# The order in which matmuls walk through their columns: blocks from the end, in an attention and softplus-MLP kernel

## The chip, the cores and the metric

The kernel runs on one core of one Trainium2 chip. The metric is the device time of one execution, in microseconds, as the median of several runs. Beside it there is one profiled execution, from which every duration below is read.

## What is computed

```python
# q, k, v: (8, 8, 576, 64); g_norm: (64,); w_in: (512, 2048); w_out: (2048, 512); all float32
kv  = einsum('bhsd,bhse->bhde', k, v)
out = einsum('bhsd,bhde->bhse', q, kv)
out = out / sqrt(mean(out * out, axis=-1) + 1e-06) * g_norm
x = out.transpose(0, 2, 1, 3).reshape(8 * 576, 512)      # 4608 tokens x 512
h = x @ w_in
g = softplus(h)                                          # max(h, 0) + log1p(exp(-|h|))
result = g @ w_out                                       # 4608 x 512
```

The attention part is small. Nearly all the arithmetic is in the two products of the MLP, 4608 x 512 x 2048 each.

## The kernel before, in words

Every float32 operand of the two large products is split into three float32r pieces (a high part, the rest scaled up, and a correction), and a product of two such operands is made by three matmuls that add into the same PSUM bank. Each matmul has a weight load of its own: 128 rows by 128 columns of the one operand are loaded into TensorE, and the columns of the other (256, 384 or 512 of them) are streamed past, read from SBUF and added into as many places of a PSUM bank. In the profile the first is LDWEIGHTS (engine PEld) and the second MATMUL (engine PE).

The work has two parts, and both take part of the 2048 middle columns, which stand in 16 chunks of 128.

The *narrow part* (up to about 355 us) goes over 12 blocks of 384 tokens while the attention is still being made. `step(s)` takes one block and one chunk: 64 steps, 4 chunks for each of the first four blocks and 6 for each of the others. `mm1` (L863) makes the 384 columns of h with 12 matmuls: 3 pieces, and for each 4 tiles of the 512 inner values. They all add into one bank, and the loop counter `m` runs from 0 to 11. Softplus and the split into pieces follow on ScalarE and VectorE, and `mm2(i)` (L870) makes the second product, for each of 3 token tiles 3 matmuls of 512 columns.

The *wide part* (from about 338 us to the end) goes over 9 blocks of 512 tokens and takes the other chunks in pairs, 48 wide steps in two phases. `wide_step(k)` makes the first product by a scheme of 7 products in place of 8, each of them on a half of 256 tokens: `product(u, q)` (L1065) has 6 matmuls of 256 columns, 3 pieces (`m`) by 2 inner tiles (`kd`), and adds into a quarter of two banks (`place(q)`). So there are 48 x 7 x 6 = 2016 matmuls of 256 columns. `mm2(c, i)` (L1136) makes the second product, 2 chunks x 4 token tiles x 3 pieces of 512 columns in each wide step, 1152 matmuls in all. Between these stand copies, softplus and splits on ScalarE and VectorE.

The order of all work is made by a planner (`Plan`): every piece of work is a task with an engine, a cost written by hand, a position, and the buffers that it takes and gives. `Plan.order` plays this through and issues the tasks in the order of the starts that it finds. A product is one task of 710 ns, an `mm2` one of 700, an `mm1` one of 2100. These costs don't depend on the way in which a matmul reads its columns.

In the kernel before, only the 256-column products read their columns in an order of their own. `from_the_end` turns an operand of n words into blocks of 4 words and takes the last block first; inside a block the words go forward. It is put on the streamed operand and on the place in PSUM alike, so each column still adds into its own place, and the sum is the same:

```python
return x.rearrange("p (b w) -> p b w", w=4)[:, ::-1]
```

All other matmuls read forward.

Of the kernel before, what the change touches and what calls it, by code (L numbers as in the profile page):

```python
# [9 lines left out]
F32R = mybir.dt.float32r  # L10
# [8 lines left out]
P = 128  # L19
# [19 lines left out]
    return x.rearrange(f"r ({' '.join(names)}) -> r {' '.join(names)}", **dict(zip(names, shape[1:])))  # L39


def from_the_end(x):

    return x.rearrange("p (b w) -> p b w", w=4)[:, ::-1]


class Slot:
# [13 lines left out]
class Plan:  # L61
# [19 lines left out]
    def slot(self, ring):  # L81
        return Slot(ring)

    def add(self, engine, ns, run, after=(), pos=0.0, take=(), give=(), size=0, behind=None, follows=None, kind="all"):
        pos, behind = round(pos, 4), None if behind is None else round(behind, 4)
        t = Task(engine, ns, run, [a for a in after if a is not None], pos, list(take), list(give), size)
        for s in t.give:
            s.readers += 1
        self.tasks.append(t)
        t.follows = follows  # L90
        t.behind = behind
        t.kind = kind
        return t
# [113 lines left out]
def kernel(  # L207
# [24 lines left out]
    nc = tc.nc  # L232
# [5 lines left out]
    KD, KF = d_model // P, d_ff // P  # L238
# [610 lines left out]
    def step(s):  # L849
        n, c = ORDER[s]  # L850
        cs = CHUNKS[n]
        h, g, gv = slot("h"), slot("g"), slot("gv")
        if c == cs[0]:
            sums[:] = [slot(f"s{i}") for i in range(TB)]
        xv, w_in, w_out = xv_slots[n], w_slots[0, c], w_slots[1, c]
        mine = list(sums)
        kept = c >= 4

        def mm1():
            hp = new(h, [P, NT])  # L860
            for m in range(3 * KD):
                i, kd = divmod(m, KD)
                nc.tensor.matmul(hp, lhsT=w_in.tile[:, i, kd * P:(kd + 1) * P], rhs=xv.tile[:, i, kd],  # L863
                                 start=(m == 0), stop=(m == 3 * KD - 1))

        def mm2(i):
            if c == cs[0]:
                new(mine[i], [P, d_model])
            for m in range(3):
                nc.tensor.matmul(mine[i].tile, lhsT=gv.tile[:, m, i * P:(i + 1) * P], rhs=w_out.tile[:, m],  # L870
                                 start=(c == cs[0] and m == 0), stop=(c == cs[-1] and m == 2))

        def low():
            nc.vector.tensor_tensor(out=gv.tile[:, 1], in0=g.tile, in1=gv.tile.bitcast(F32)[:, 0], op=ALU.subtract)

        def less():
            f32 = gv.tile.bitcast(F32)
            nc.vector.scalar_tensor_tensor(out=gv.tile[:, 2], in0=f32[:, 1], scalar=-RADIX, in1=f32[:, 0],
                                           op0=ALU.mult, op1=ALU.add)

        a = add("PE", 2100, mm1, x_split[n] + factors_done[0, c] + [m for _, m in mm1s[-1:]] +
                (factors_done[1, ORDER[s - 2][1]] if s > 1 else []), s, [h],
                ([xv] if c == cs[-1] else []) + ([w_in] if s == last_step[c] and c != 4 else []))
        mm1s.append((s, a))
        a = add("ACT", 490, lambda: nc.scalar.activation(new(g, [P, NT]), h.tile, func=AF.Softplus, scale=1.0 + E),  # L885
                [a], s, [g], [h])
        a = add("ACT", 530, lambda: nc.scalar.activation(new(gv, [P, 3, NT], F32R)[:, 0], g.tile, func=AF.Copy, scale=DOWN),
                [a], s, [gv])
        a = add("DVE", 570, low, [a], s, [], [g])
        a = add("DVE", 570, less, [a], s)  # L890
        for i in range(TB):
            a2 = add("PE", 700, lambda i=i: mm2(i), [a] + factors_done[1, c] + [mm2s.get(i)], s + 1.5,
                     [mine[i]] if c == cs[0] else [],
                     [gv] + ([w_out] if s == last_step[c] and not kept else []))
            mm2s[i] = a2
            if c == cs[-1]:
                leave(0, n * TB + i, mine[i], a2, s + 1.5)
# [145 lines left out]
    def wide_step(k):  # L1043
        ph, n, p = STEPS[k]
        ab, gv = slot("ab"), slot("gvp")
        b = starts[k]
# [3 lines left out]
        mine = list(wide_sums)  # L1050
        outs = [w_slots[1, c] for c in (2 * p, 2 * p + 1)]

        def place(q):
            return ab.tile[:, q // 2, q % 2 * HW:(q % 2 + 1) * HW]
# [3 lines left out]
        def product(u, q):  # L1058
            f, i = PRODUCTS[u]
            w = forms[p][f].tile  # L1060
            dst, v = unit_slots[ph, n, u]
            for m in range(3):
                for kd in range(2):
                    at = i * 2 * P + kd * P
                    nc.tensor.matmul(from_the_end(place(q)), lhsT=w[:, m, at:at + P],  # L1065
                                     rhs=from_the_end(dst.tile[:, m, v, kd] if u < 6 else dst.tile[:, m, kd]),
                                     start=(u == 0 and not m and not kd), stop=(m == 2 and kd == 1), skip_group_check=True)

        def multiply(u, q, after, pos, take=(), follows=None):
            f = PRODUCTS[u][0]  # L1070
            give = [unit_slots[ph, n, u][0]] if last else []
            if final and u in (2, 3, 5, 6):
                give.append(forms[p][f])
            return add("PE", 710, lambda: product(u, q), unit_done[ph, n, u] + forms_done[p][f] + list(after), pos, take, give,
                       follows=follows)
# [3 lines left out]
        def gt(dtype=F32):  # L1079
            if dtype not in held:  # L1080
                held[dtype] = sb.tile([P, 2, WIDE], dtype, tag=f"g{gv.place}", name=f"g{gv.place}_{dtype == F32}")
            return held[dtype]

        def gvt(m, dtype=F32):
            y = gv.tile[:, m]
            return y if dtype == F32R else y.bitcast(F32)
# [8 lines left out]
        def begin():  # L1095
            new(ab, None)
            product(0, X)
# [33 lines left out]
        def mm2(c, i):  # L1131
            fresh = first and not c and ph < LAST
            if fresh:
                new(mine[i], [P, d_model])
            for m in range(3):
                nc.tensor.matmul(mine[i].tile, lhsT=(gvt(m, F32R) if m < 2 else gt(F32R))[:, c, i * P:(i + 1) * P], rhs=outs[c].tile[:, m],  # L1136
                                 start=fresh and not m, stop=(last and c == 1 and m == 2), skip_group_check=True)

        seeds = {}
# [19 lines left out]
        for c in range(2):  # L1159
            for i in range(TW):  # L1160
                slot_pos = b + PACE + MM2[TW * c + i]
                a2 = add("PE", 700, lambda c=c, i=i: mm2(c, i),
                         [split_done[c]] + factors_done[1, 2 * p + c] + ([seeds[i]] if i in seeds and not c else []) +
                         ([before[i]] if c or not first else []), slot_pos, [mine[i]] if first and not c and ph < LAST else [], [gv] + ([outs[c]] if final else []))
                before[i] = a2
                if last and c:
                    leave(ph, TW * n + i, mine[i], a2, slot_pos)
# [98 lines left out]
```

## Time and profile before

| what | value |
|---|---|
| median of 3 runs | 866.39 us (864.64 to 867.66) |
| profiled execution | 864.34 us |
| its span, first to last instruction | 862.5 us |
| granted TensorE clock, mean | 0.999 |
| matmuls of 256 columns (L1065) | 2016 |
| matmuls of 512 columns, wide part (L1136) | 1152 |
| matmuls of 384 columns (L863) | 768 |
| matmuls of 512 columns, narrow part (L870) | 576 |

A matmul's row in the profile (281 ns for 256 columns, 389 for 512) begins when it starts to stream and ends when its last result is there. The next one starts to stream long before that, so rows overlap. What a matmul costs is the distance from its start to the next one's start.

### The profile page before, as it was taken

What the parts mean: (1) busy time and instruction counts of PE and PEld (TensorE: products, weight loads), DVE (VectorE), ACT (ScalarE), POOL (GpSimd) and SP (SyncE); (2) the same over time, 40 slices, a digit from 0 to 9 for tenths busy, and PEclk for the clock granted to TensorE, in tenths of its full rate; (3) what the DMA queues carried; (4) which work ended last, traced back from release to release, by engine and by line L of the source; (5) the groups of instructions that cost most, each with busy time, mean ns of one, the idle gap of its engine ahead of it and who ended that gap; (6) DMA issues with size and microseconds to landing.
All of it is one profiled execution on the core that took longest, in us unless ns stands there. A gap on an engine that the chain in (4) does not pass through costs nothing.

```text
span 862.5 us, 17080 instructions
## 1 busy us (share of the span) xinstructions
PE 849.7 (99%) x6464; PEld 757.7 (88%) x6464; DVE 704.6 (82%) x995; ACT 521.2 (60%) x980; POOL 76.1 (9%) x79
## 2 busy tenths in 40 slices
PE   8899999999999999999999999999999999999998
PEld 5578888898888999999999999998999899999996
DVE  7988898888788888798888788878788766788873
ACT  6866664436354467766667665654868555566654
POOL 0342223111113300000000000000000000000000
PEclk9999999999999999999999999999999999999999
DMA  9998997779784655436645546645364753778863
GB/s 285 283 234 222 261 263 242 178 235 226 210 188 118 188 157 183 141 107 216 199 158 164 166 154 205 190 158 176 123 196 138 232 165 102 244 234 240 247 187 130
DMA packets 239778, 167.07 MB, mean 194 GB/s; under 512 B 106320, under 2 KB 198736, under 8 KB 239696
## 3 DMA queue, kind: packets, MB, share of 16 engines
q1 hardware_dynamic: 239392, 165.86, 65.7%
q8 instruction: 50, 0.82, 0.4%
q14 instruction: 32, 0.26, 0.1%
q10 hardware_dynamic: 304, 0.13, 0.1%
HBM read 112.98 MB, written 52.95 MB: 192 GB/s over the span
## 4 chain that ended last, share of the span: by engine, by line
PE 94%; DVE 1%; ACT 1%; POOL 0%; issue 0%; ACTq 0%; DVEq 0%
PE banks L1136 30%; PE banks L1065 28%; PE banks L870 16%; PE banks L863 15%; PE banks L720 2%; PE banks L696 2%; PE banks L738 0%; DVE units L643 0%; DVE half L732 0%; PE banks L1230 0%; POOL roots L728 0%; DVE units L646 0%; DVE roots L724 0%; DVE m L464 0%; ACT units L640 0%
## 5 line engine op out<-in xcount | busy, mean ns | idle before, releaser
L1136 PE MATMUL banks<-pieces,gv 128*128 128x512 f32 x768 | 238.0, 391 | 0.0
L1136 PE MATMUL banks<-pieces,g_False 128*128 128x512 f32 x384 | 149.4, 389 | 0.0
L1136 PEld LDWEIGHTS banks<-pieces,gv 128*128 128x128 f32 x768 | 132.5, 188 | 17.3
L863 PE MATMUL banks<-units,pieces 128*128 128x384 f32 x768 | 145.4, 337 | 0.0
L870 PE MATMUL banks<-pieces,gv 128*128 128x512 f32 x576 | 144.9, 396 | 0.0
L863 PEld LDWEIGHTS banks<-units,pieces 128*128 128x128 f32 x768 | 135.5, 188 | 4.9
L870 PEld LDWEIGHTS banks<-pieces,gv 128*128 128x128 f32 x576 | 106.1, 188 | 20.3
L1065 PEld LDWEIGHTS banks<-units,pieces 128*128 128x128 f32 x840 | 112.0, 188 | 6.5 <-ACT banks L1111 0.4
L1065 PE MATMUL banks<-units,pieces 128*128 128x256 f32 x840 | 116.4, 282 | 0.0
L885 ACT ACTIVATE half<-banks 128x384 f32<-128x384 f32 x64 | 31.5, 492 | 97.3 <-PE banks L863 97.1
L1126 DVE TENSOR_TENSOR gv<-g_True,gv 128x1024 fp32r<-128x1024 f32 x47 | 57.5, 1224 | 36.5 <-ACT gv L1123 36.5
L1136 PEld LDWEIGHTS banks<-pieces,g_False 128*128 128x128 f32 x384 | 72.1, 188 | 15.7
L1065 PEld LDWEIGHTS banks<-units,w 128*128 128x128 f32 x504 | 67.3, 188 | 3.7 <-ACT banks L1111 0.2
L1065 PE MATMUL banks<-units,w 128*128 128x256 f32 x504 | 70.3, 282 | 0.0
L728 POOL TENSOR_TENSOR roots<-roots,half 128x8 f32<-128x8 f32 x36 | 62.2, 1727 | 3.0
L1129 DVE SCALAR_TENSOR_TENSOR g_False<-gv 128x1024 fp32r<-128x1024 f32 x47 | 57.6, 1225 | 1.5
L1028 DVE TENSOR_TENSOR units<-loads,units 128x1024 fp32r<-128x1024 f32 x42 | 51.2, 1219 | 6.2 <-ACT units L1025 6.1
L1093 ACT ACTIVATE g_True<-banks 128x256 f32<-128x256 f32 x96 | 36.7, 383 | 31.6 <-PE banks L1065 31.0
L1115 DVE TENSOR_TENSOR g_True<-banks,g_True 128x512 f32<-128x512 f32 x48 | 33.2, 691 | 27.7 <-PE banks L1065 22.5
L930 ACT ACTIVATE m<-banks 128x512 f32<-128x512 f32 x72 | 42.1, 595 | 18.7 <-PE banks L1136 12.8
L1031 DVE SCALAR_TENSOR_TENSOR units<-units 128x1024 fp32r<-128x1024 f32 x42 | 51.4, 1224 | 1.8
L1025 ACT ACTIVATE units<-loads 128x1024 fp32r<-128x1024 f32 x42 | 44.5, 1059 | 12.4 <-PE banks L1065 8.9
(115 smaller groups left out, 1250.2 us busy)
## 6 DMA issues: line engine op xcount, KB each, us to landing
loads<-x SPq DMA_DIRECT2D x180, 128.0 KB, 2.7
part<-m SPq DMA_DIRECT2D x72, 256.0 KB, 2.9
m<-part SPq DMA_DIRECT2D x72, 256.0 KB, 3.3
loads<-form SPq DMA_DIRECT2D x45, 256.0 KB, 3.3
form<-loads SPq DMA_DIRECT2D x36, 256.0 KB, 3.1
raw<-in_moe_w_in_dram SPq DMA_DIRECT2D x16, 512.0 KB, 4.8
loads<-in_k_dram SPq DMA_DIRECT2D x32, 256.0 KB, 4.4
loads<-in_v_dram SPq DMA_DIRECT2D x32, 256.0 KB, 4.6
```

The lines of the kernel that those rows point to most:

```text
L728: nc.gpsimd.tensor_tensor(out=r.tile, in0=r.tile, in1=half, op=ALU.pow)
L863: nc.tensor.matmul(hp, lhsT=w_in.tile[:, i, kd * P:(kd + 1) * P], rhs=xv.tile[:, i, kd], start=(m == 0), stop=(m == 3 * KD - 1))
L870: nc.tensor.matmul(mine[i].tile, lhsT=gv.tile[:, m, i * P:(i + 1) * P], rhs=w_out.tile[:, m], start=(c == cs[0] and m == 0), stop=(c == cs ...
L930: a = add("ACT", 690 if ph == LAST else 600, lambda: nc.scalar.activation(new(ot, [P, d_model]), bank.tile, func=AF.Copy, scale=scale if p ...
L1025: nc.scalar.activation(part_of(0, F32R), xl.tile if m > 1 else xl.tile[:, 0], func=AF.Copy, scale=DOWN)
L1028: nc.vector.tensor_tensor(out=part_of(1, F32R), in0=xl.tile if m > 1 else xl.tile[:, 0], in1=part_of(0), op=ALU.subtract)
L1031: nc.vector.scalar_tensor_tensor(out=part_of(2, F32R), in0=part_of(1), scalar=-RADIX, in1=part_of(0), op0=ALU.mult, op1=ALU.add)
L1065: nc.tensor.matmul(from_the_end(place(q)), lhsT=w[:, m, at:at + P], rhs=from_the_end(dst.tile[:, m, v, kd] if u < 6 else dst.tile[:, m, kd ...
L1093: nc.scalar.activation(dst, src, func=AF.Softplus, scale=1.0 + E)
L1126: nc.vector.tensor_tensor(out=gvt(1, F32R), in0=gt(), in1=gvt(0), op=ALU.subtract)
L1129: nc.vector.scalar_tensor_tensor(out=gt(F32R), in0=gvt(1), scalar=-RADIX, in1=gvt(0), op0=ALU.mult, op1=ALU.add)
L1136: nc.tensor.matmul(mine[i].tile, lhsT=(gvt(m, F32R) if m < 2 else gt(F32R))[:, c, i * P:(i + 1) * P], rhs=outs[c].tile[:, m], start=fresh ...
```

## The change

`from_the_end` gets the size of its blocks as an argument, and leaves the operand as it is where that is 0. It is then used in three places, on both sides of the matmul each time:

- the 256-column products: blocks of 16 words where `kd` is 0 and of 8 words where it is 1, in place of 4 for both;
- the 512-column matmuls of the wide part (L1136): pieces of 128 words, the last piece first, in place of forward;
- the last of the 12 matmuls of each `mm1` (L863): single words, so that the 384 columns go from the last to the first. The other eleven stay forward.

The 512-column matmuls of the narrow part (L870) stay as they were. Two lines are added ahead of them, so L863 is L864 in the changed kernel, L870 is L871, L1065 is L1066 and L1136 is L1137.

```diff
-def from_the_end(x):
-
-    return x.rearrange("p (b w) -> p b w", w=4)[:, ::-1]
+def from_the_end(x, w):
+
+    return x.rearrange("p (b w) -> p b w", w=w)[:, ::-1] if w else x
...
             for m in range(3 * KD):
                 i, kd = divmod(m, KD)
-                nc.tensor.matmul(hp, lhsT=w_in.tile[:, i, kd * P:(kd + 1) * P], rhs=xv.tile[:, i, kd],
+                w = 1 if m == 3 * KD - 1 else 0
+                nc.tensor.matmul(from_the_end(hp, w), lhsT=w_in.tile[:, i, kd * P:(kd + 1) * P], rhs=from_the_end(xv.tile[:, i, kd], w),
                                  start=(m == 0), stop=(m == 3 * KD - 1))
...
             for m in range(3):
                 for kd in range(2):
                     at = i * 2 * P + kd * P
-                    nc.tensor.matmul(from_the_end(place(q)), lhsT=w[:, m, at:at + P],
-                                     rhs=from_the_end(dst.tile[:, m, v, kd] if u < 6 else dst.tile[:, m, kd]),
+                    nc.tensor.matmul(from_the_end(place(q), (16, 8)[kd]), lhsT=w[:, m, at:at + P],
+                                     rhs=from_the_end(dst.tile[:, m, v, kd] if u < 6 else dst.tile[:, m, kd], (16, 8)[kd]),
                                      start=(u == 0 and not m and not kd), stop=(m == 2 and kd == 1), skip_group_check=True)
...
             for m in range(3):
-                nc.tensor.matmul(mine[i].tile, lhsT=(gvt(m, F32R) if m < 2 else gt(F32R))[:, c, i * P:(i + 1) * P], rhs=outs[c].tile[:, m],
+                nc.tensor.matmul(from_the_end(mine[i].tile, P), lhsT=(gvt(m, F32R) if m < 2 else gt(F32R))[:, c, i * P:(i + 1) * P],
+                                 rhs=from_the_end(outs[c].tile[:, m], P),
                                  start=fresh and not m, stop=(last and c == 1 and m == 2), skip_group_check=True)
```

## The prediction

> **What bounds the kernel now.** I read the page first: shares of the engines, then the chain of work that ended last.
>
> ```profile
> span 862.5 us, 17080 instructions
> PE 849.7 (99%) x6464; PEld 757.7 (88%) x6464; DVE 704.6 (82%) x995; ACT 521.2 (60%) x980; POOL 76.1 (9%) x79
> ...
> PEclk9999999999999999999999999999999999999999
> ...
> PE 94%; DVE 1%; ACT 1%; POOL 0%; issue 0%; ACTq 0%; DVEq 0%
> ```
>
> TensorE is the bound from end to end: 94% of the chain is matmuls, the granted clock is full in every slice. So a nanosecond taken from each matmul of a group comes off the span one for one, and one added is paid one for one. The answer on what TensorE waited for adds up to some 8 us, all of it on lines of the first part of the run; there is no wait in the part with the 256-column products that could hide a longer product.
>
> The next question is what one matmul costs. A matmul's own row (281 ns for 256 columns) is no help, since matmuls overlap; what counts is the distance from one start to the next. The chain in order of time, for two stretches, gives it.
>
> ```profile
> 503.81 2.84 PE banks L1065 x24
> 506.65 2.72 PE banks L1136 x12
> 509.37 0.71 PE banks L1065 x6
> 510.08 2.05 PE banks L1136 x9
> ```
>
> ```profile
> 250.51 2.10 PE banks L863 x12
> 252.62 2.08 PE banks L870 x9
> ```
>
> Columns: start, length, what, how many. 2.84 us for 24 is 118.3 ns for a product of 256 columns (L1065), 2.72 for 12 is 226.7 ns for 512 columns (L1136), 2.10 for 12 is 175 ns for 384 (L863), 2.08 for 9 is 231 ns for 512 in the narrow part (L870). Starts of single matmuls show more. In an undisturbed row of wide ones they are 226, 227, 227 ns apart, in an undisturbed row of 384-column ones 173, 173, 174. So 128 more columns cost 53.3 ns, a column 0.417 ns, and streaming alone would be 213.3, 160.0 and 106.7 ns for 512, 384 and 256 columns. What is left is a gap of 13.4 ns a matmul where the columns are read forward. The products, which alone are read last block first (blocks of 4 words), have 118.3 - 106.7 = 11.6 ns. Read forward they should cost 106.7 + 13.4 = 120.1 ns.
>
> The third view is the timeline of TensorE around a change from products to wide matmuls.
>
> ```profile
> 509.21 0.87 PE L1065 MATMUL banks<-units,w 128*128 128x256 f32 x6
> 509.92 0.63 PE L1136 MATMUL banks<-pieces,gv 128*128 128x512 f32 x2
> 510.38 0.39 PE L1136 MATMUL banks<-pieces,g_False 128*128 128x512 f32 x1
> 510.61 0.62 PE L1136 MATMUL banks<-pieces,gv 128*128 128x512 f32 x2
> ```
>
> The six products in the first row start 118, 116, 123, 116, 118 and 117 ns before the next. The two wide matmuls behind them take 235 and 230 ns (510.38 - 509.92 is 0.46), those after them 226 or 227 (511.06 - 510.61 is 0.45). The same figures come back in every such place, whatever ACT, DVE or the DMAs do at that moment: the gap belongs to how one matmul's columns follow another's. In the products the long ones are the even matmuls of a six (kd = 0; mean 120.2 ns over the run) and the short ones the odd (kd = 1; 116.3). The narrow part behaves alike: after twelve 384-column matmuls, nine L870 run 229, 233, 236, 224, 231, 235, 229, 232, 231 ns apart before they settle, and the next twelve begin 171, 175, 177, 185, 176, 182 before 173. No wait stands in these rows.
>
> **The change, part by part.** It adds and removes no instruction of work and changes no order: on all engines the same operations stand in the same order, with a few semaphore waits of DVE and ACT grouped otherwise. Planner costs, DMAs, tiles and numbers of columns are untouched. Only the sequence in which 3,232 matmuls walk through their columns, in SBUF and in PSUM alike, is new. So no row of before prices it; each term is bounded by nearest rows.
>
> *Products, L1065.* 48 wide steps of 7 products of 6 matmuls: 2,016, half of them (kd = 0) in blocks of 16 words, half in blocks of 8. Best end: every product at the shortest start-to-start seen, 115.5 ns: 2.8 x 2,016 = 5.6 us gained. Worst end: every one like the long ones, 123 ns: 4.7 x 2,016 = 9.5 us lost. With forward behaviour, 120.1 ns, it is 1.8 x 2,016 = 3.6 us lost. I take 117.0: the odd half stays at 116.3, and the even half, which alone carries the excess and whose neighbours now walk in another block size than it does, loses two thirds of its 3.9 ns. That is 1.3 x 2,016 = 2.6 us gained.
>
> *Wide matmuls, L1136.* 48 x 2 x 4 x 3 = 1,152, now four pieces of 128 columns, last piece first. Their chain share, 30.4% of 862.5 us, is 262.2 us, 227.6 ns each. Best end: 223.3 ns, the gap of 10 ns that the odd products have: 4.3 x 1,152 = 5.0 us gained. Worst: all at 235.5 ns, as the first behind a six: 7.9 x 1,152 = 9.1 us lost. Within a piece the columns go forward, so I take little: 1.3 ns, 1.5 us gained, about what the 235 and 231 cases cost now (106 of the first and 83 of the second: 0.9 + 0.4 us).
>
> *Every twelfth 384-column matmul, L863.* 64 of them, read word by word from the end. Their own price: 160 ns more each if a step backward by one word streams at half rate, 10.2 us lost; nothing if it streams at full rate, as blocks of 4 words do (a product's row is 281 ns and a wide one's 389: the difference of 108 is 256 columns at full rate). What follows may change: L870 has 233.6 ns a matmul by its chain share (15.6%, 576), 6.9 over the settled 226.7, 4.0 us in all, and the six unsettled L863 behind it some 20 ns a time, about 1 us. If the backward one resets the state, up to 5 us come back; I take a fifth, 0.9 us, with full rate for the matmul itself, since it is nearest to the block rows.
>
> The PSUM — Partial Sum Buffer page of the Trainium skill (Specifications) says that PSUM lines are 8 bytes and that any access which is not contiguous slows matmuls significantly. The trace has 16-byte runs, backward, with no such slowing (118.3 against 120.1 ns). Taken as it stands, the rule would put the one-word backward matmuls at the slow end of the third term.
>
> The page TensorE: Matmul & The Clock Gate (Back-to-back issue gap) has N/2.4 + 2.5 ns, 109 ns for 256 columns. The trace disagrees with 118.3; by the page, an order that removed the whole difference would gain an estimated 18 us, and no row here comes near it.
>
> Sum: 2.6 + 1.5 + 0.9 = 5.0 us. The profiled execution took 864.34 us, 1.8 more than its span; the median of the three runs is 866.39. Off the median: 861.4 us; a profile after would show a span of about 857.5.
>
> **Rivals.**
> 1. Long blocks read like forward reading: runs of 16 and 8 words are nearer to an ascending stream than runs of 4, and the small gap of the products goes back to 13.4 ns. Place: L1065. Price 3.6 us, with nothing gained at L1136: 870.0 us, slower. For it: the only backward reading in the trace is the only one with a smaller gap. Against: half of the products already show more gap than the other half with the same blocks, so the neighbour matters, not the block alone. It decides as soon as the mean of L1065 is over 119.6 ns, where its loss passes 2.6 us.
> 2. One-word steps stream at half rate: 10.2 us at L863, less the 4.1 of the two other terms: 872.5 us, slower. For it: no row steps by one word backward. Against: four such words still lie side by side. It decides from some 105 ns a matmul (64 x 105 = 6.7 us).
> 3. The order does not matter: the gap comes from the weight load that each matmul has (one LDWEIGHTS each, 188 ns a row, x6464 on both). 866.4 us. Against: products differ from forward matmuls by 1.8 ns with the same weight loads.
>
> **How the numbers follow.** Forecast 0.57, rival 1 0.20, rival 2 0.11, rival 3 0.12. A difference under 0.3% (2.6 us) cannot be told from none here. So faster 0.57, same 0.12, slower 0.31. The likeliest case by itself runs from 854 (the first two terms at their best ends, 5.6 + 5.0 us, and 1.8 us of the third) to 863.8; the range goes on to 873.0 to take in both slow rivals, and leaves out the worst ends at L1065 and L1136.
>
> **What would show it.** Right: in the chain after, 24 products in about 2.81 us or less, 12 wide ones in 2.70 or less, the L870 rows nearer to 227 ns, L863 rows of the backward ones at 334 ns like the others. Rival 1: 24 products in 2.88. Rival 2: one row of twelve at L863 near 490 ns. Wrong altogether: a wait in front of TensorE in the wide part, or a granted clock under 1.0.

## The result, and the profile after

The changed kernel takes 859.41 us (858.61 to 861.46, 6 runs) against 865.72 us (864.64 to 867.66, 6 runs): a ratio of 0.9933, 95% interval 0.9919 to 0.9947. It is faster by 6.3 us. The forecast was 861.4 us with a range of 854.0 to 873.0. The profiled execution took 858.61 us.

From the page after:

```profile
span 856.8 us, 17075 instructions
...
PE 843.8 (98%) x6464; PEld 754.7 (88%) x6464; DVE 704.1 (82%) x995; ACT 520.2 (61%) x980; POOL 76.1 (9%) x79
...
PE 94%; DVE 2%; ACT 1%; DMA 1%; issue 1%; POOL 1%; SPq 0%; DVEq 0%; ACTq 0%
```

The span is 5.7 us shorter, the same 6464 matmuls are on TensorE, and it still carries 94% of the chain. The chain in order of time, in the wide part and in the narrow part (start, length, what, how many):

```profile
500.94 2.80 PE banks L1066 x24
503.74 2.72 PE banks L1137 x12
506.46 0.70 PE banks L1066 x6
507.16 2.04 PE banks L1137 x9
```

```profile
249.32 2.11 PE banks L864 x12
251.43 2.04 PE banks L871 x9
```

24 products take 2.80 us (2.84 before), 116.7 ns each. Twelve wide matmuls take 2.72 us as before, but nine of them behind only six products take 2.04 in place of 2.05, and the nine L871 take 2.04 in place of 2.08. Twelve 384-column matmuls have not become shorter (2.11, 2.10 before). The timeline of TensorE at the change from products to wide ones:

```profile
506.30 0.86 PE L1066 MATMUL banks<-units,w 128*128 128x256 f32 x6
507.00 0.62 PE L1137 MATMUL banks<-pieces,gv 128*128 128x512 f32 x2
507.45 0.39 PE L1137 MATMUL banks<-pieces,g_False 128*128 128x512 f32 x1
507.68 0.62 PE L1137 MATMUL banks<-pieces,gv 128*128 128x512 f32 x2
```

The six products stand 116, 117, 117, 116, 117, 117 ns apart, and the first two wide ones take 0.45 us (507.45 - 507.00), not 0.46. The 235 and 230 ns have become 227 and 227.

Over the whole trace, the mean distance from a matmul's start to the next start, by line:

| matmuls | before, ns | after, ns | gained, us |
|---|---|---|---|
| 256 columns, 2016 | 118.3 | 116.9 | 2.8 |
| 512 columns, wide part, 1152 | 228.0 | 227.1 | 1.1 |
| 512 columns, narrow part, 576 | 236.2 | 233.3 | 1.7 |
| 384 columns, 768 | 178.0 | 178.0 | 0.0 |

The gain is the count times the difference of the unrounded means; the sum is 5.6 of the 5.7 us. (These means hold the few waits too, so they lie above the settled distances.) What changed is how many are settled, that is, stand at the distance that an undisturbed row ends up with: of the 2016 products, 982 stood 116 or 117 ns apart before and 1894 do so after; of the 576 L870 (L871 after), 115 stood at 226 to 228 ns before and 451 after.

### The profile page after: what moved, and what is told of

The parts are those of the page before. It is cut to its first block, busy times and chain, and to the rows that moved or that the text cites. A ratio compares the mean times of both kernels' runs of the same rounds, so it can differ in the third digit from the quotient of the medians.

```text
span 856.8 us, 17075 instructions
## 1 busy us (share of the span) xinstructions
PE 843.8 (98%) x6464; PEld 754.7 (88%) x6464; DVE 704.1 (82%) x995; ACT 520.2 (61%) x980; POOL 76.1 (9%) x79
## 4 chain that ended last, share of the span: by engine, by line
PE 94%; DVE 2%; ACT 1%; DMA 1%; issue 1%; POOL 1%; SPq 0%; DVEq 0%; ACTq 0%
PE banks L1137 31%; PE banks L1066 28%; PE banks L871 16%; PE banks L864 15%; PE banks L720 2%; PE banks L696 2%; DMA loads<-in_v_dram 1%; DMA raw<-in_moe_w_in_dram 0%; PE banks L738 0%; POOL roots L728 0%; PE banks L1232 0%; DVE half L732 0%; DVE m L464 0%; DVE m L460 0%; DVE units L643 0%
## 5 line engine op out<-in xcount | busy, mean ns | idle before, releaser
L1137 PE MATMUL banks<-pieces,gv 128*128 128x512 f32 x768 | 236.8, 390 | 0.0
L1137 PE MATMUL banks<-pieces,g_False 128*128 128x512 f32 x384 | 149.4, 389 | 0.0
L1137 PEld LDWEIGHTS banks<-pieces,gv 128*128 128x128 f32 x768 | 132.5, 188 | 17.2 <-DVE banks L910 0.2
L864 PE MATMUL banks<-units,pieces 128*128 128x384 f32 x768 | 145.6, 338 | 0.0
L871 PE MATMUL banks<-pieces,gv 128*128 128x512 f32 x576 | 143.3, 393 | 0.0
L864 PEld LDWEIGHTS banks<-units,pieces 128*128 128x128 f32 x768 | 135.5, 188 | 4.5
L871 PEld LDWEIGHTS banks<-pieces,gv 128*128 128x128 f32 x576 | 106.2, 188 | 19.0
L1066 PEld LDWEIGHTS banks<-units,pieces 128*128 128x128 f32 x840 | 111.0, 188 | 6.5 <-ACT banks L1112 0.4
L1066 PE MATMUL banks<-units,pieces 128*128 128x256 f32 x840 | 115.2, 280 | 0.0
L1137 PEld LDWEIGHTS banks<-pieces,g_False 128*128 128x128 f32 x384 | 72.1, 188 | 15.0
L1066 PEld LDWEIGHTS banks<-units,w 128*128 128x128 f32 x504 | 66.7, 188 | 3.7 <-ACT banks L1112 0.2
L1066 PE MATMUL banks<-units,w 128*128 128x256 f32 x504 | 69.6, 280 | 0.0
```

What stands on the lines that cost most here:

```text
L864: nc.tensor.matmul(from_the_end(hp, w), lhsT=w_in.tile[:, i, kd * P:(kd + 1) * P], rhs=from_the_end(xv.tile[:, i, kd], w), start=(m == 0), ...
L1066: nc.tensor.matmul(from_the_end(place(q), (16, 8)[kd]), lhsT=w[:, m, at:at + P], rhs=from_the_end(dst.tile[:, m, v, kd] if u < 6 else dst. ...
L1137: nc.tensor.matmul(from_the_end(mine[i].tile, P), lhsT=(gvt(m, F32R) if m < 2 else gt(F32R))[:, c, i * P:(i + 1) * P], rhs=from_the_end(ou ...
```

## Experiments: one part at a time

Two theories stood at the start. "Own line": each of the three edits acts on its own matmuls and on the few behind them. "Combination": the matmuls settle only when all the orders fit. Four kernels took the parts by themselves, or went forward everywhere. (Line numbers are those of the changed kernel, and each edit shown is against it unless the text says otherwise.)

**Products alone.**

```diff
-                w = 1 if m == 3 * KD - 1 else 0
+                w = 0 if m == 3 * KD - 1 else 0
...
-                nc.tensor.matmul(from_the_end(mine[i].tile, P), lhsT=(gvt(m, F32R) if m < 2 else gt(F32R))[:, c, i * P:(i + 1) * P],
-                                 rhs=from_the_end(outs[c].tile[:, m], P),
+                nc.tensor.matmul(from_the_end(mine[i].tile, 0), lhsT=(gvt(m, F32R) if m < 2 else gt(F32R))[:, c, i * P:(i + 1) * P],
+                                 rhs=from_the_end(outs[c].tile[:, m], 0),
```

> Of the change, only the products: blocks of 16 and 8 words by turns; the wide matmuls and the last 384-column one forward as before. Theory 'own line' (each edit acts on its own matmuls and on the few behind them): products at 116.7 ns start to start as in the changed kernel (118.3 before), 24 of them in 2.80 us; wide ones at most at 227.6 ns; L871 still unsettled at about 234 ns. Span about 3.2 us under before, ratio about 0.996. Rival 'combination' (products settle only because the wide matmuls ahead of them end in another piece): products stay at 118 ns and the ratio at 1.000.

Measured: 861.91 us, ratio 0.9969 (0.9956 to 0.9981). The chain in the wide part:

```profile
503.00 2.80 PE banks L1066 x24
505.80 2.72 PE banks L1137 x12
508.52 0.70 PE banks L1066 x6
509.22 2.04 PE banks L1137 x9
```

This is the wide part of the changed kernel, to the last figure, with wide matmuls that go forward. The nine behind six products are at 2.04 us too: products by turns leave the wide ones settled. By the trace this kernel gains 2.8 us at the products and 1.1 us at the wide ones. Nine L871 take 2.08 us as before.

**Pieces alone.** Products in blocks of 4, the twelfth forward, the wide ones in pieces.

> Of the change, only the wide matmuls: four pieces of 128 columns, last piece first; products in blocks of 4, the last 384-column one forward. Theory 'own line': the 235 and 231 ns behind six products go, 0.5 to 1.5 us gained, settled wide ones stay at 226.7 ns, products at 118.3. Ratio 0.998 to 0.9995. Rival 'combination': nothing at L1137, since the unsettled ones come from the products ahead of them: ratio 1.000; or products settle too, ratio 0.995.

Measured: 865.69 us, ratio 1.0012 (1.0003 to 1.0021): no gain, if anything a loss. The chain has the same lengths as before, with the unsettled nine behind six products:

```profile
509.35 0.71 PE banks L1066 x6
510.05 2.05 PE banks L1137 x9
```

**The backward twelfth alone.** Products in blocks of 4, the wide ones forward, `w = 1` for the last of twelve.

> Of the change, only the last of twelve 384-column matmuls backward, word by word. Theory 'own line': its own cost stays 173 ns (337 ns row, 334 for the others), and the nine L871 behind it run 227 ns apart instead of 229, 233, 236: 1.5 to 2 us gained, ratio 0.998; products and wide ones as before. Rival 'half rate': a row near 490 ns, and a loss of 10 us. Rival 'combination': L871 stays at 234 ns.

Measured: 862.88 us, ratio 0.9981 (0.9972 to 0.9990). The chain in the narrow part:

```profile
247.00 2.11 PE banks L864 x12
249.11 2.04 PE banks L871 x9
```

The nine behind are 228, 227, 226, 227, ... ns apart, 0.04 us less a time. The backward one itself has a row of 337 ns where its neighbours have 334, and the next start comes 173 or 174 ns later, as with the others. In the changed kernel the rows of the line say the same: were single backward words read at half rate, the 64 backward rows would stand near 490, and the nine at the top (422 to 446) are first ones behind transposes and attention matmuls, and nine such stood there before (421 to 446).

```profile
L864 PE MATMUL banks<-units,pieces x768: 333/334/446, 43.8 to 350.4; 128*128 128x384 f32 x192
```

**All forward.**

> Every matmul forward, products too. By the working of the prediction a forward product costs 106.7 + 13.4 = 120.1 ns start to start, so 24 in 2.88 us, 3.6 us over before, ratio about 1.004. Rival: the gap of products does not come from the direction (weight loads); they stay at 118.3 ns and the ratio at 1.000.

Measured: 869.04 us, ratio 1.0054 (1.0042 to 1.0067).

```profile
505.11 2.87 PE banks L1066 x24
507.98 2.75 PE banks L1137 x12
```

Forward products settle at 120.0 ns, the 106.7 + 13.4 of the prediction. Their mean is 119.3, 1.0 over before (2.1 us), and the wide ones behind them are less settled than before: 233, 236, 228, 233, 231, a mean of 230.1 against 228.0 (2.4 us).

**The changed kernel without pieces**, which tells whether the pieces count together with the rest:

> The changed kernel with its wide matmuls forward again; products by turns and the backward twelfth stay. Theory 'pieces do nothing' (wide matmuls in pieces of 128 were unsettled behind products in blocks of 4 just as forward ones are): the time of the changed kernel, ratio to before 0.993 to 0.995, wide ones at 226.7 ns. Rival 'combination' (the two other parts alone add up to 0.5%, the whole is 0.67%): ratio 0.995 and over, with wide ones or products unsettled.

Measured: 859.65 us, ratio 0.9939 (0.9927 to 0.9951), within the interval of the changed kernel. So no gain of the pieces is shown, alone or together. Products alone and the twelfth alone give 0.31% and 0.19%, 0.50% in all, and both together 0.61%; the intervals overlap, and a combination beyond the sum is not shown. The traces add up without one: 2.8 and 1.1 us in the kernel with the products alone and 1.7 us at L871 in that with the twelfth alone make the 5.6 us of the changed kernel. (The spans of single profiles blur this: in that of the twelfth alone, 862.5 us as before, the L776 transposes of the first part took 1.7 us longer.)

## Experiments: what it is about the order

**Which memory.** Two kernels put the turned blocks on one side only; `from_the_end(..., 0)` leaves an operand forward.

```diff
-                    nc.tensor.matmul(from_the_end(place(q), (16, 8)[kd]), lhsT=w[:, m, at:at + P],
+                    nc.tensor.matmul(from_the_end(place(q), 0), lhsT=w[:, m, at:at + P],
```

> The changed kernel, but the 256-column products take only their streamed operand in blocks from the end (16 and 8 by turns) and add into PSUM forward; so columns land in other places and the output is another one, with the same work. Theory 'reading side' (the gap comes from how SBUF is read): 116.7 ns start to start, as in the changed kernel. Theory 'adding side' (it comes from how PSUM is walked): settled at 120.0 ns, as the products that go forward on both sides.

```diff
-                                     rhs=from_the_end(dst.tile[:, m, v, kd] if u < 6 else dst.tile[:, m, kd], (16, 8)[kd]),
+                                     rhs=from_the_end(dst.tile[:, m, v, kd] if u < 6 else dst.tile[:, m, kd], 0),
```

> The mirror image: the products read their streamed operand forward and walk PSUM in blocks from the end (16 and 8 by turns); columns land in other places, the work is the same. Theory 'reading side': 120.0 ns. Theory 'adding side': 116.7 ns. If both this and its mirror image stand at 120, both sides are needed; if neither does, either one is enough.

The chain of the first, blocks on the streamed operand in SBUF:

```profile
502.52 2.80 PE banks L1066 x24
```

and of the second, blocks in PSUM:

```profile
504.01 2.87 PE banks L1066 x24
506.88 2.75 PE banks L1137 x12
```

The first has the distances of the changed kernel (116.7 ns), the second those of all forward (120.0, with the wide ones unsettled). One run each: 860.3 and 867.72 us. For the products and the wide matmuls behind them it is the reading of the streamed operand from SBUF that counts; walking PSUM in blocks of 16 and 8 words neither helps nor costs. The rule of the Trainium skill weighed in the prediction (PSUM — Partial Sum Buffer, Specifications) does not show in these matmuls: blocks in PSUM left the products at the forward distance, and behind the twelfth, which walks PSUM backward by single words, the next start comes after 173 or 174 ns as before. For blocks of 16 and 8 in longer streams the two sides were not separated (see the kernel with turns everywhere).

**Which sizes.** Blocks of 16 in all products, and blocks of 8 in all.

> The changed kernel with blocks of 16 words in all products, in place of 16 and 8 by turns. Theory 'neighbours' (the gap depends on a matmul's order against that of the one before it): not settled at 116.7; between 117 and 120 ns, with a pattern as with blocks of 4, ratio to before 0.995 to 0.999. Rival 'block size' (any block over 4 words will do): 116.7 ns and the ratio of the changed kernel, 0.993.

> The changed kernel with blocks of 8 words in all products. Theory 'neighbours' (two different sizes by turns are what settles them): unsettled, 117.5 to 120 ns as with 4 and 16 alone. Rival 'eight is the size': 116.7 ns as with 16 and 8 by turns.

The chain with 16 in all (864.90 us, ratio 0.9995, 0.9986 to 1.0005):

```profile
504.26 2.84 PE banks L1066 x24
```

and with 8 in all (one run, 869.35 us):

```profile
505.29 2.88 PE banks L1066 x24
```

With 8 alone the products settle at 120.0 ns, as if they went forward; with 16 alone they run 116, 118, 119 ns over and over (mean 118.2), with 4 alone 118, 117, 122, 116 (118.3). Only by turns do they stand at 116.7. So neither size brings the gain by itself; the two by turns do. 16 and 8 is the only pair that was tried. The ratio with 16 in all lies above the expected 0.995 to 0.999, since the wide ones behind these products are less settled than before (a mean of 229.3 ns against 228.0, 1.4 us).

**Turns everywhere.** The same turns in the 384- and 512-column matmuls.

```diff
-                w = 1 if m == 3 * KD - 1 else 0
+                w = (16, 8)[m % 2]
...
-                nc.tensor.matmul(mine[i].tile, lhsT=gv.tile[:, m, i * P:(i + 1) * P], rhs=w_out.tile[:, m],
+                nc.tensor.matmul(from_the_end(mine[i].tile, (16, 8)[(i + m) % 2]), lhsT=gv.tile[:, m, i * P:(i + 1) * P], rhs=from_the_end(w_out.tile[:, m], (16, 8)[(i + m) % 2]),
...
-                nc.tensor.matmul(from_the_end(mine[i].tile, P), lhsT=(gvt(m, F32R) if m < 2 else gt(F32R))[:, c, i * P:(i + 1) * P],
-                                 rhs=from_the_end(outs[c].tile[:, m], P),
+                nc.tensor.matmul(from_the_end(mine[i].tile, (16, 8)[(i + m) % 2]), lhsT=(gvt(m, F32R) if m < 2 else gt(F32R))[:, c, i * P:(i + 1) * P],
+                                 rhs=from_the_end(outs[c].tile[:, m], (16, 8)[(i + m) % 2]),
```

> Turns of 16 and 8 everywhere: also in all 384-column matmuls (by m) and in all 512-column ones of both parts (by i + m), in place of pieces of 128 and of one backward matmul in twelve. Theory 'gap of 10 by turns' (two neighbours in different block sizes leave 10 ns whatever their number of columns): 170.0 ns for 384 and 223.3 ns for 512 columns, 768 x 3.3 + 1728 x 3.3 = 8.2 us under the changed kernel at best, ratio to before about 0.984. Rival 'only where columns are 256' (10 ns belongs to a length at which the weight load, 128 columns, is as long as the stream): 173.3 and 226.7 ns as before, ratio about 0.993; or unsettled, over 0.995.

Measured: 877.26 us, ratio 1.0140 (1.0121 to 1.0158). Both theories missed: it is slower than all forward. A wide matmul's own row has grown from 389 to 396 ns:

```profile
L1137 PE MATMUL banks<-pieces,g_False x384: 396/396/401, 371.7 to 870.7; 128*128 128x512 f32 x192
```

They stand 231 to 237 ns apart (226.7 before), and the 384-column ones 174 and 179 by turns (173.3), with a row of 338 ns in place of 334. In these longer streams the blocks cost time inside the stream; whether in SBUF or in PSUM was not separated. The products between the wide ones lose their 116.7 too:

```profile
509.50 2.88 PE banks L1066 x24
```

They keep their blocks of 16 and 8 by turns in this kernel, and yet 24 of them take 2.88 us, 120.0 ns each: 116, 118, 121, 122, 121, 122 in each six, over and over. So turns of neighbours are not enough: they bring 116.7 only together with what stands around the products. In the wide part the wide matmuls are all that differs from the changed kernel, so the way in which they walk seems to tell through all 24 products. How it does stays open.

**A backward last one in the narrow part's 512-column matmuls too**, as a way to a faster version:

```diff
-                nc.tensor.matmul(mine[i].tile, lhsT=gv.tile[:, m, i * P:(i + 1) * P], rhs=w_out.tile[:, m],
+                w = 1 if (i, m) == (2, 2) else 0
+                nc.tensor.matmul(from_the_end(mine[i].tile, w), lhsT=gv.tile[:, m, i * P:(i + 1) * P], rhs=from_the_end(w_out.tile[:, m], w),
```

> The changed kernel, and the last of the nine 512-column matmuls of a narrow step (i = 2, m = 2) backward as well, word by word. Theory 'a backward last one settles what follows': the six L864 behind it at 173.3 ns in place of 171, 175, 177, 185, 176, 182, which is 26 ns less in some 50 places, 1.3 us; ratio to before about 0.992. Rival 'only towards longer matmuls' (it settles 512 behind 384, not 384 behind 512): L864 as before, ratio as in the changed kernel.

Measured: 859.22 us, ratio 0.9941 (0.9926 to 0.9956): no difference from the changed kernel.

```profile
247.39 2.05 PE banks L872 x9
249.44 2.11 PE banks L864 x12
```

The six behind (line L864 still; L871 is L872 here) stay at 172, 175, 177, 185, 176, 182, and the backward ninth costs 232 ns in place of 227. What settles 512 columns behind 384 does not settle 384 behind 512.

**The weight load.** All matmuls forward, products with every second word as weights (the edit is against the kernel with all forward).

```diff
-                    nc.tensor.matmul(from_the_end(place(q), 0), lhsT=w[:, m, at:at + P],
+                    nc.tensor.matmul(from_the_end(place(q), 0), lhsT=w[:, m, i * 2 * P + kd:(i + 1) * 2 * P:2],
```

> All matmuls forward, as in the kernel with every matmul forward, but the products load every second word of 256 as their weights in place of 128 in a row; so the weights are other ones, in the same number, and the output is another. Theory 'two reads' (the gap of 13.4 ns comes from the weight load and the streamed operand being read from SBUF at the same time): the products leave 120.0 ns, more likely upwards. Theory 'stream alone' (the gap lies in how one streamed operand follows the other): 120.0 ns, as with weights in a row.

One run, 871.52 us. The weight loads of products, here and then in the kernel with all forward:

```profile
L1066 PEld LDWEIGHTS banks<-units,pieces x840: 193/195/202, 358.7 to 856.0; 128*128 128x128 f32 x168
```

```profile
L1066 PEld LDWEIGHTS banks<-units,pieces x840: 187/192/192, 356.4 to 853.2; 128*128 128x128 f32 x168
```

The loads take 195 ns in place of 192, but the products still stand 120 ns apart for the most part (mean 119.5 against 119.3). Neither theory comes out clean: the distance stayed, as "stream alone" has it, yet the settling did not, and the load's own row moves with the way that the streamed operand is read (188 ns with blocks by turns, 192 forward). But the load's row and the distance don't go together: with blocks of 8 in all products the row is 188 ns as well, and the products stand 120.0 ns apart. Whether the two reads disturb each other stays open.

## Why the prediction was right

**The bound and the exchange rate.** A nanosecond a matmul came off one for one: the table's 5.6 us are the span's 5.7, and no wait took its place: the 1% of DMA that is new in the chain is a matter of the first loads, where TensorE waits 2.1 us for the v loads in place of 1.2. (The part with the products was not quite free of waits: three weight loads waited 0.6 us in all, before and after alike.) Right.

**Products: 2.6 us forecast, 117.0 ns.** With the products alone changed, their mean distance was 116.9 ns, 2.8 us less over the 2016 of them by the trace. (The 0.31% of that kernel, 2.7 us with an interval of 0.19% to 0.44%, holds the gain of the wide matmuls too.) The size was right, the picture only in part: the odd half was to stay at 116.3 and the even half to come down. In fact both came to nearly the same mean, the even half down from 120.2 to 117.0 and the odd half up from 116.4 to 116.8.

**Wide matmuls: 1.5 us forecast, by the pieces.** The 235 and 231 ns behind products did go, worth 1.1 us in the trace after, but not by the pieces, which gained nothing alone or together. They went because the products ahead read by turns, as the products alone show. The term's cause was wrong, the saving belonged to the first edit, and that its size nearly held is luck. The sign named for it, twelve wide ones in 2.70 us or less, did not come: they take 2.72 as before.

**The twelfth: 0.9 us forecast.** The mechanism was right (the backward one is read at full rate and resets the state), and the term was mis-sized: a fifth of 5 us was taken, and alone it measured 0.19%, 1.6 us (0.10% to 0.28%). Where L871 stand directly behind the twelve, they settle wholly, and the 1.7 us of the trace after are all that the unsettled ones cost there. The 4.0 us that were thought to be there, taken from a mean, held other things too: above all single long distances of 314 ns and more beside other work, and some 0.3 us behind attention matmuls (L720), where rows stay unsettled (229, 234, 236, 224, 231). The 1 us at the six L863 behind them did not come at all.

**Rivals.** Rival 1 had its distance right, 120.0 ns, and its place: with blocks of 8 in all products it is what happens. Its reason, that longer blocks come nearer to forward reading, does not hold: with the longer blocks of 16 the mean is 118.2. The turns are what kept it away, as "the neighbour matters, not the block alone" had it; but the nearest neighbour is not all either, as turns everywhere show. Rival 2 is out: 337 ns a row, not 490. Rival 3 is out as it stands: five orders of the products gave distances from 116.7 to 120.0 ns with the same number of weight loads. How much of the 10 ns that are left belongs to the weight load no run shows.

What stays open is the cause below that: why one streamed read behind another leaves 10 ns with 16 and 8 by turns, some 11.5 with blocks of 4 or of 16 alone and 13.3 with blocks of 8 alone or forward, why the same turns leave 13.3 when the wide ones read by turns too, and why the state after a change of length lasts six or more matmuls. For the products, and for the wide ones behind them, the runs show that it is on the SBUF side and does not hang on PSUM; for the backward twelfth the two sides were not separated.

## What to carry to other kernels

Where TensorE is the bound, subtract the columns' own time from the distance between starts (not from a matmul's row), and look at the distances one by one: a pattern that comes back whatever the other engines do is a cost of its own, here up to 7% of a matmul (185 ns for 173), and the order in which the streamed operand is read can move it. Take each edit by itself before crediting it: of three, one did nothing that could be measured and its forecast gain belonged to another. And such an order is no rule to spread: the turns that gained 0.3% on the 256-column products made the kernel 1.4% slower than before when put on all matmuls.

## What the runs showed that I had not expected

- Single words backward, 384 of them, stream at full rate in SBUF and PSUM: a row of 337 ns against 334, and the next start after 173 or 174 ns.
- Blocks of 16 and 8 words by turns, on both sides, slow a stream of 512 columns (396 against 389 ns a row) and not one of 256 (280 in the changed kernel against 281 before).
- With 8-word blocks in every product the distance is the forward one, 120.0 ns; with 16 and 8 by turns it is 116.7, and 120.0 again when the wide matmuls read by turns too.
- A change in how products read moved matmuls that were not changed: the wide ones behind six products, from 235 and 230 ns to 227.
